# LN on ScalarE, bias loads on another queue, deferred h stores and four late dO products in a transformer block's backward kernel

## The chip, the cores and the metric

The kernel runs on one core of one Trainium2 chip. The metric is the device time of one execution in microseconds, lower is better; it is given as the median of several runs. One further execution is recorded by the hardware profiler, and all profile lines come from it.

## The reference

The kernel computes the forward result and all gradients of a small gated block. With S = 2048 rows, D = 512, 32 heads of 16 and F = 1792, in bfloat16:

```python
xn = layernorm(x)
s = attention(xn; wqkv, wo)                  # 32 heads, full softmax, then @ wo
y = layernorm(xn)
h = gelu(y @ w1 + b1); m = h @ w2 + b2
out = x + s * silu(m)
# outputs: out and the gradients of x, wqkv, wo, w1, b1, w2, b2 for a given grad_out
```

The layer norm is applied twice, so there are two sets of row means and deviations. The gradient that enters the attention is `(grad_out * silu(m)) @ wo.T`; the kernel calls the factor before the product `dso` and the product dO.

## The kernel before

Line numbers are those of the profile. Everything runs in an order that is written out by hand: each engine (and each engine's DMA queue) takes its instructions in program order, and an instruction that has to wait holds up those behind it. There are three phases: `phase_pre` (L38), `attention_core` (L637) and `phase3`. The change touches the first, and the first block of the second. Tensors have 16 row tiles of 128 rows; four tiles make a group.

**QKV stage of `phase_pre`.** SP (SyncE's queue) loads `x_all` in four groups (L74). ACT's queue loads `wqkv` in three parts (L76), w1 (L77), b1 (L78, two-byte elements spread over partitions) and b2 (L79, broadcast to 128 partitions). `stats` takes the moments of a group on DVE (VectorE: L86, L87), the square root on ACT (ScalarE: L89), the reciprocal and -mean/deviation on DVE (L90, L91). `norm` (L96) normalises four tiles on DVE. `ln1(g)` makes `xn` from `x` and transposes it into `xnT`: group 0 through PE (TensorE), the others by a DMA transpose on SP (L111). `ln2(g)` makes `y` from `xn` and a transpose `yT` (L118).

The loop over 16 tiles does, per tile t: three products of `xnT` with `wqkv_sb` (L139), each in one of six PSUM buffers; three casts to SBUF on ACT (L144 to L146) into `NSall` (two buffers of four tiles) and `NQ`; two squares on POOL (GpSimd, L150); then, if t is in `hooks`, one LN step, ln1(2), ln1(3), ln2(0) to ln2(3) after tiles 1, 3, 5, 8, 11, 14; then the reduction of the previous tile's squares on DVE (L125). After every fourth tile SP stores `NSall` and `NQ` to DRAM (`NAT_s`, `NATQq_s`, L157, L158).

**h1.** `h1(sc)` makes the hidden layer for one group: 14 groups of four matmuls (L185), the bias added on DVE into an `h1row` buffer (L188, six buffers), the GELU on ACT into `hgT` (L189), and a store of `h1row` to `H1T_s` on SP (L190). At its end SP stores the whole `hgT`, 1.8 MB, to `HGT_s` (L191). The order is `h1(0)`, load of `w2_sb` (L254), `load_dot(0)` (L178), transposing load of `woT` (L256), `h1(1)`, `load_dot(1)`, `row_bound`, then the sixteen `m_step`s, with `h1(2)` and `h1(3)` after the first and second four.

**`m_step(t)`** has a pipeline of six tiles: transposes of `dso(t-2)` on PE (`dso_tr`, L225) and their copy on ACT (L227), the product with `woT` for tile t-5 (`proj`, L233) and its copy into `ND` on ACT (L235), `gate(t-1)` and `slope_out(t-3)` on DVE and POOL (L206 to L219), and the 14 matmuls of m (L197) for tile t. After tile 15 come the last transposes and `proj(11)` to `proj(15)`.

**Attention.** 16 pairs of heads times four query blocks, 64 blocks, each of 16 steps; the backward half of a block runs during the next block, so the first block has none. A step has scores `s` (L758), `d` (L770), an exponential on ACT (L784), two products on DVE (L802), and the accumulations into `X` (L828, L840, L852); from the second block on also `t` (L744) with its exponential (L792) and `Z` (L924, L936). `eg` buffers rotate by three, each written for four steps and then transposed by a DMA (L813). The pair-0 operands for query tiles 4 to 15 are loaded and transposed during block 0, in steps 1, 3 and 5.

## Time and profile before

| what | us |
|---|---|
| median of four runs | 2346.89 (2340.46 to 2358.44) |
| the profiled execution | 2340.46 |
| its span | 2338.4 |
| PE busy in the span | 2175.6 (93%) |
| ACT busy | 1834.6 (78%) |
| DVE busy | 1805.0 (77%) |
| POOL busy | 1196.5 (51%) |
| attention's first score matmul starts at | 202.72 |

The page divides the span into 40 slices; shares over the whole span are mostly those of the long attention phase. For the first part one has to look at the stretches: a table by stage gives each engine's busy time there, and the clock that the throttle granted to TensorE (1.00 is full speed). A line of the instructions in order of time gives start, duration, engine, source line, operation, output and input; in brackets stand the idle time before it and what ended it. "SPq" and "ACTq" are the DMA issues of these engines, and their time is that of the issue, not of the transfer. PE's busy time is modelled and includes the overlap of neighbouring matmuls.

### The profile page before, as it was taken

To read this page: it belongs to the slowest core of one execution; us is meant where nothing else is said; L and a number is where in the kernel's file an instruction comes from. 1 tells how busy PE (TensorE), PEld (TensorE's weight loads), DVE (VectorE), ACT (ScalarE), POOL (GpSimd) and SP (SyncE) were. 2 spreads that over 40 slices of the span, in tenths; PEclk is the share of its full clock that TensorE was granted. 3 is DMA by queue.
4 is the path that set the end of the run, shared out by engine and by line. 5 is a ranking of instruction groups with operands and counts; after the bars stand their busy time and mean duration, and the time that the engine had idled before them with its cause. 6 is when DMAs were issued, how large, how long until landed. Compare 5 with 4: busy or idle time off the path is not lost.

```text
span 2338.4 us, 47577 instructions
## 1 busy us (share of the span) xinstructions
PE 2175.6 (93%) x18320; PEld 729.8 (31%) x18320; DVE 1805.0 (77%) x3022; ACT 1834.6 (78%) x2131; POOL 1196.5 (51%) x1956
## 2 busy tenths in 40 slices
PE   6799999999999999999999999999999998789997
PEld 2343222222222222222222222222222223234455
DVE  7676698998999899978888998998888994204641
ACT  4555799999999999989999999999998995221231
POOL 4247447566575657465656656474756555200020
PEclk9997699999999999989999999999998999999999
DMA  7867799999999999999999999999999999898556
GB/s 197 246 210 192 179 240 240 236 250 247 230 248 243 242 234 249 245 214 236 245 242 245 248 247 249 245 240 244 243 223 229 239 236 244 213 234 244 163 81 129
DMA packets 1761557, 529.90 MB, mean 227 GB/s; under 512 B 1682337, under 2 KB 1746994, under 8 KB 1761330
## 3 DMA queue, kind: packets, MB, share of 16 engines
q1 hardware_dynamic: 1715858, 467.59, 98.2%
q10 hardware_dynamic: 33152, 31.87, 4.9%
q0 software_dynamic: 12320, 27.41, 4.0%
q8 instruction: 143, 2.34, 0.4%
q14 instruction: 84, 0.69, 0.1%
HBM read 47.98 MB, written 58.33 MB: 45 GB/s over the span
## 4 chain that ended last, share of the span: by engine, by line
PE 51%; ACT 23%; DMA 10%; POOL 6%; DVE 4%; issue 4%; ACTq 1%; SPq 0%; POOLq 0%; DVEq 0%
ACT e L792 11%; ACT eg L784 10%; PE d L770 9%; PE s L758 8%; PE X L828 8%; DMA tg<-eg 5%; PE X L840 4%; PE Z L936 3%; PE X L852 2%; PE ps_dhg L551 2%; PE ps_h L185 2%; PE ps_dy L566 2%; DMA hgc<-HGT_s 1%; PE ps_dw L625 1%; PE ps_m L197 1%
## 5 line engine op out<-in xcount | busy, mean ns | idle before, releaser
L802 DVE TENSOR_TENSOR eg<-d,eg 128x512 bf16<-128x512 f32 x2048 | 1349.5, 688 | 186.0 <-PE d L770 69.8
L784 ACT ACTIVATE eg<-s 128x1024 bf16<-128x1024 f32 x1024 | 1041.3, 1034 | 72.3 <-PE d L770 54.6
L770 PE MATMUL d<-QDT,KVT 32*128 32x512 bf16 x2048 | 807.6, 394 | 0.7 <-DVE eg L802 0.6
L792 ACT ACTIVATE e<-t 128x1024 bf16<-128x1024 f32 x640 | 662.9, 1036 | 44.0 <-PE t L744 41.7
L758 PE MATMUL s<-QDT,KVT 32*128 32x512 bf16 x2048 | 409.6, 395 | 42.2 <-ACT eg L784 39.5
L840 PE MATMUL X<-eg,NAT 128*32 128x512 bf16 x2048 | 414.9, 402 | 0.0
L828 PE MATMUL X<-eg,Lc 128*32 128x512 bf16 x2048 | 414.8, 402 | 0.0
L852 PE MATMUL X<-eg,NAT 128*17 128x512 bf16 x2048 | 407.9, 395 | 0.0
L770 PEld LDWEIGHTS <-KVT 32*128 32x128 bf16 x2048 | 186.0, 91 | 347.2 <-issue 347.2
L924 PE MATMUL Z<-e,W 128*32 128x512 bf16 x1280 | 256.5, 396 | 20.7 <-POOL W L891 19.4
L744 PE MATMUL t<-KVT,QDT 32*128 32x512 bf16 x1280 | 254.5, 391 | 3.1 <-ACT eg L784 2.7
L758 PEld LDWEIGHTS <-KVT 32*128 32x128 bf16 x2048 | 116.8, 91 | 296.2 <-issue 294.4
L936 PE MATMUL Z<-tg,W 128*32 128x512 bf16 x2048 | 207.6, 390 | 0.0
L885 POOL TENSOR_TENSOR W<-NATQd,rL 128x128 bf16<-128x128 bf16 x64 | 25.9, 405 | 350.4 <-DVE rL L869 350.4
L828 PEld LDWEIGHTS <-Lc 128*32 128x32 bf16 x2048 | 98.8, 93 | 285.5 <-issue 285.5
L691 POOL TENSOR_TENSOR bg_v<-bg_t 128x512 f32<-128x512 f32 x56 | 58.0, 1036 | 193.6 <-ACT bg_t L706 193.2
L924 PE MATMUL Z<-tg,W 128*32 128x512 bf16 x768 | 154.5, 399 | 0.0
L840 PEld LDWEIGHTS <-NAT 128*32 128x32 bf16 x2048 | 99.1, 94 | 168.0 <-issue 168.0
L342 POOL TENSOR_TENSOR dx<-lnb_prod,lnb_dy 128x512 bf16<-128x512 f32 x16 | 20.9, 1312 | 233.0 <-DVE lnb_prod L341 233.0
L950 DVE TENSOR_TENSOR acc<-Z,acc 128x512 f32<-128x512 f32 x192 | 130.7, 681 | 10.5 <-PE Z L936 10.5
L924 PEld LDWEIGHTS <-W 128*32 128x32 bf16 x2048 | 108.9, 93 | 47.4 <-POOL W L891 23.7
L852 PEld LDWEIGHTS <-NAT 128*17 128x17 bf16 x2048 | 92.9, 88 | 60.3 <-issue 60.3
(164 smaller groups left out, 2749.4 us busy)
## 6 DMA issues: line engine op xcount, KB each, us to landing
H1T_s<-h1row SPq DMA_DIRECT2D x56, 128.0 KB, 1.8
HGT_s<-hgT SPq DMA_DIRECT2D x4, 1792.0 KB, 7.9
bg_x<-H1T_s POOLq DMA_DIRECT2D x56, 128.0 KB, 5.4
GP_s<-bg_m POOLq DMA_DIRECT2D x56, 128.0 KB, 5.5
gp<-GP_s ACTq DMA_DIRECT2D x8, 896.0 KB, 7.1
DH1T_s<-dh1T SPq DMA_DIRECT2D x4, 1792.0 KB, 9.6
NAT_s<-NSall SPq DMA_DIRECT2D x4, 1056.0 KB, 6.5
NAT<-NAT_s POOLq DMA_DIRECT2D x16, 264.0 KB, 5.9
```

The costliest lines, as they stand in the source:

```text
L744: nc.tensor.matmul(t[:, hj, :], lhsT=op["QDT"][r:r + 32, q0:q0 + 128], rhs=op["KVT"][r:r + 32, kc * 512:(kc + 1) * 512], start=True, stop= ...
L758: nc.tensor.matmul(s[:, hj, :], lhsT=op["KVT"][r:r + 32, kb * 128:(kb + 1) * 128], rhs=op["QDT"][r:r + 32, qc * 512:(qc + 1) * 512], start ...
L770: nc.tensor.matmul(d[:], lhsT=op["KVT"][r:r + 32, kb * 128:(kb + 1) * 128], rhs=op["QDT"][r:r + 32, qc * 512:(qc + 1) * 512], start=True, ...
L784: nc.scalar.activation(out=cur["eg"][1][:, :, kb % 4, :, :].rearrange("k b h q -> k h b q"), in_=st_s.pop(g)[:].rearrange("k h (b q) -> k ...
L792: nc.scalar.activation(out=e[:], in_=st_t.pop(g)[:], func=ACT.Exp)
L802: nc.vector.tensor_tensor(out=gts[:, kb % 4, hj, :].rearrange("k (b q) -> k b q", b=4), in0=ds[hj][:].rearrange("k (b q) -> k b q", b=4), ...
L828: nc.tensor.matmul(X[64 + 32 * hj:96 + 32 * hj, :], lhsT=Lc[:], rhs=et[:, :, kb % 4, hj, :], start=(kb == 0), stop=False, skip_group_check ...
L840: nc.tensor.matmul(X[32 * hj:32 * hj + 32, :], lhsT=NATt[:, kb, hj, 1:33], rhs=et[:, :, kb % 4, hj, :], start=(kb == 0), stop=(kb == 15), ...
L852: nc.tensor.matmul(X[64 + 32 * hj:64 + 32 * hj + 17, :], lhsT=NATt[:, kb, hj, 0:17], rhs=gts[:, kb % 4, hj, :], start=False, stop=(kb == 1 ...
L924: nc.tensor.matmul(Z[32 * hj:32 * hj + 32, :], lhsT=blk[j]["W1"][:, qb, hj, :], rhs=ev[:, hj], start=(i == 0), stop=False, tile_position=( ...
L936: nc.tensor.matmul(Z[c:c + 32, :], lhsT=blk[j]["W2"][:, qb, hj, :], rhs=gv[:, :, hj, qb, :], start=(i == 1), stop=(i >= 2), tile_position= ...
L950: nc.vector.tensor_tensor(out=av, in0=Z[:], in1=av, op=ALU.add)
```

## The change

- `norm_act` normalises on ACT, as `x * rstd + nmr` with both taken per row. It serves all groups of `ln2`, and groups 1 to 3 of `ln1`; group 0 stays on DVE. `ln2` works in place in `xn`, whose buffers go from four to three. The hooks are ln1(2), ln2(0), ln1(3), ln2(1), ln2(2), ln2(3) after tiles 1, 3, 5, 8, 11, 14.
- The loads of b1 and b2 leave ACT's queue. With the loads of `w2_sb` and `woT` they're put on SP after tile 5 of the QKV loop.
- The store of `hgT` becomes `store_h`, called after the next `h1` for groups 0 to 2, and before the last `gate` for group 3. `h1row` has eight buffers; the squares' buffers go from four to three.
- The three 16 KB `eg` buffers of the attention are made before `phase_pre`, each with a name of its own. `phase_pre` uses them first: `x_all`, then `hgT` of groups 0 and 2, in the first; `hgT` of groups 1 and 3 in the second; `w1_sb`, then `late_sb`, in the third. `late_sb` holds a second transposed copy of `wo` (loaded on SP after `h1(3)`), the `ND` buffer and transposes for tiles 12 to 15, and `dso(15)`. `NSall` moves to the pool of the QKV stage.
- `proj(12)` to `proj(15)` and `dso_tr(15)` become a generator `rest` that the attention loop calls in its first steps; they use the PSUM buffer of `Z`. The loads of the pair-0 operands in block 0 move from steps 1, 3, 5 to 7, 9, 11.

```diff
+LATE = 12
...
+        eg_as = lambda i, shape, name: k.egp.tile(shape, bf16, name=name, tag=f"eg{i}")
-        x_all = hp.tile([128, NT, D], bf16, name="x_all", tag="hA")
-        NSall = hp.tile([128, 2, NPAIR, 4, 2, NATW], bf16, name="NSall", tag="hB")
-        w1_sb = hp.tile([128, IC, F], bf16, name="w1_sb")
+        x_all = eg_as(0, [128, NT, D], "x_all")
+        w1_sb = eg_as(2, [128, IC, F], "w1_sb")
...
-            nc.scalar.dma_start(out=b1_bf[:], in_=B_b1.rearrange("(c p) -> p c", p=128))
-            nc.scalar.dma_start(out=b2_bf[:], in_=B_b2.rearrange("(o d) -> o d", o=1).to_broadcast([128, D]))
...
+            def norm_act(dst, src, g, rstd_all, nmr_all):
+                for i in range(4):
+                    t = 4 * g + i
+                    nc.scalar.activation(out=dst[:, i, :], in_=src[:, i, :], func=ACT.Identity, bias=nmr_all[:, t:t + 1], scale=rstd_all[:, t:t + 1])
...
-                xn[g] = p0.tile([128, 4, D], bf16, name="xn", bufs=4)
-                norm(nc.vector, xn[g], src, mv, rs)
+                xn[g] = p0.tile([128, 4, D], bf16, name="xn", bufs=3)
                 if g == 0:
+                    norm(xn[g], src, mv, rs)
...
                 else:
+                    norm_act(xn[g], src, g, k.rstd1, k.nmr1)
...
-                y[g] = p0.tile([128, 4, D], bf16, name="y", bufs=2)
-                norm(nc.vector, y[g], xn[g], mv, rs)
+                norm_act(xn[g], xn[g], g, k.rstd2, k.nmr2)
...
-                    sq = wk0.tile([128, H, DH], f32, name="sq", bufs=4)
+                    sq = wk0.tile([128, H, DH], f32, name="sq", bufs=3)
...
+                if t in hooks:
+                    hooks[t]()
+                if t == 5:
+                    nc.sync.dma_start(out=b1_bf[:], in_=B_b1.rearrange("(c p) -> p c", p=128))
+                    nc.sync.dma_start(out=b2_bf[:], in_=B_b2.rearrange("(o d) -> o d", o=1).to_broadcast([128, D]))
+                    nc.sync.dma_start(out=w2_sb[:], in_=B_w2.rearrange("(c p) d -> p c d", p=128))
+                    nc.sync.dma_start_transpose(out=woT[:], in_=A_wo)
...
-                    h1row = hp.tile([128, 512], bf16, name="h1row", bufs=6)
+                    h1row = hp.tile([128, 512], bf16, name="h1row", bufs=8)
...
+            def store_h(sc):
                 nc.sync.dma_start(out=k.HGT_s[:, sc * 512:(sc + 1) * 512].rearrange("(c p) s -> p c s", p=128), in_=hgs[sc][:])
...
             h1(0)
-            nc.sync.dma_start(out=w2_sb[:], in_=B_w2.rearrange("(c p) d -> p c d", p=128))
             load_dot(0)
-            nc.sync.dma_start_transpose(out=woT[:], in_=A_wo)
             h1(1)
             load_dot(1)
+            store_h(0)
             row_bound()
...
                 if sc + 2 < 4:
                     h1(sc + 2)
+                    store_h(sc + 1)
+                if sc == 1:
+                    late_sb = eg_as(2, [128, 16, IC, 128], "late_sb")
+                    nc.sync.dma_start_transpose(out=late_sb[:, 0:4].rearrange("p b m q -> p b (m q)"), in_=A_wo)
+            store_h(3)
...
-            for t in range(NT - 5, NT - 2):
+            for t in range(NT - 5, LATE):
                 proj(t)
-            dso_tr(NT - 1)
-            proj(NT - 2)
-            proj(NT - 1)
+
+            def rest(psum):
+                proj(LATE, psum([128, 512], f32))
+                yield
+                dso_tr(NT - 1, psum([128, IC, 128], bf16))
+                yield
+                for t in range(LATE + 1, NT):
+                    proj(t, psum([128, 512], f32))
+                    yield
+            return rest
...
-    late += [(1, lambda: ops0["load_d"](4, NT)), (3, lambda: ops0["cq"](4, NT)), (5, lambda: ops0["tq"](4, NT))]
+    late += [(7, lambda: ops0["load_d"](4, NT)), (9, lambda: ops0["cq"](4, NT)), (11, lambda: ops0["tq"](4, NT))]
+    rest = rest_of_pre(lambda shape, dt: ps_z.tile(shape, dt, name="Z0", tag="z"))
     emit_s(0)
     emit_exp_a(0)
...
+        if g < 7:
+            next(rest, None)
```

## The prediction

> **What bounds the kernel now.** I read four views in this order: the table by stage, the instructions in order of time over the first 112 us, the chain of work that ended last around 200 us, and the instructions of single tiles for durations. The profiled execution took 2340.46 us around a span of 2338.4 us; the median of the four runs is 2346.89 us, 6.4 us above it. All sums below are differences against the profiled execution and are then taken off the median.
>
> The first stretches are, in order: query/key/value (QKV) and LN, the two first `h1`, the sixteen `m_step`, attention block 0, block 1, block 2. Columns: PE, weight loads, DVE, ACT, POOL busy us with counts, then granted clock, DMA share, GB/s.
>
> ```profile
> 17.50:77.70 60.20, 50.59 (x233) 23.11 (x234) 56.29 (x141) 30.33 (x62) 32.33 (x32) 1.00 0.68 156
> 77.70:108.70 31.00, 22.13 (x89) 9.29 (x89) 16.98 (x25) 15.54 (x25) 0.45 (x1) 0.84 0.93 281
> 108.70:198.00 89.30, 87.90 (x450) 40.86 (x449) 67.18 (x94) 49.13 (x81) 52.22 (x54) 1.00 0.67 212
> 198.00:240.00 42.00, 39.02 (x192) 8.07 (x189) 25.01 (x38) 25.39 (x31) 20.07 (x26) 0.61 0.85 193
> 240.00:279.70 39.70, 39.70 (x248) 8.15 (x249) 24.80 (x38) 27.67 (x30) 13.98 (x25) 0.51 0.75 173
> 279.70:306.00 26.30, 25.79 (x253) 7.71 (x254) 24.06 (x39) 25.48 (x29) 13.46 (x25) 1.00 1.06 212
> ```
>
> QKV is bound by DVE (56.29 of 60.20). The `h1` stretch is bound by nothing that computes: PE works 22 of 31 us. The `m_step` stretch is bound by PE. Blocks 0 and 1 run at about half clock with PE full; block 1 takes 39.7 us where block 2 takes 26.3.
>
> ```profile
> 6.56 9.39 ACTq L79 DMA_DIRECT2D b_bf<-in_B_b_dram  x1
> 8.77 0.18 DVE L87 BATCH_NORM_AGGREGATE ln_mv<-ln_st 128x2 f32<-128x6 f32 x1
> 15.98 1.28 ACT L89 ACT_TABLE_LOAD   x1 [15.98 <-issue]
> 20.51 1.91 PE L139 MATMUL pk<-wqkv_sb,xnT 128*128 128x512 bf16 x4
> ...
> 90.27 4.71 SPq L178 DMA_DIRECT2D dot<-in_grad_out_dram  x1
> 95.03 7.07 SPq L256 DMA_TRANSPOSE woT<-in_A_wo_dram  x1
> 104.80 5.36 DVE L188 TENSOR_SCALAR h1row<-ps_h,b1c 128x512 bf16<-128x512 f32 x8 [12.39 <-DMA H1T_s<-h1row]
> 105.60 3.22 PE L185 MATMUL ps_h<-yT,w_sb 128*128 128x512 bf16 x8 [8.87 <-DVE h1row L188]
> ```
>
> Two stalls stand out. ACT issues the b2 load until 15.95, while its statistics were ready at 8.95. And SP is held by the dot and `woT` issues from 90.3 to 102.1, the `H1T_s` stores queue behind them, six `h1row` buffers run out, and PE stands for 8.87 us; its next eight matmuls take 0.40 us each instead of 0.216.
>
> **The change, part by part.**
>
> **Bias loads off ACT.** The Sqrt waits only for the statistics: end 9.4 instead of 17.58. The steps from there to the first QKV matmul take 20.51 - 17.58 = 2.9, so it starts at 12.3: 8.2 us earlier. Its inputs are there: the three `wqkv_sb` loads land within 5.4 to 8.0 us of issues that end at 2.4.
>
> **LN normalised on ACT.** Seven of eight groups leave DVE: 7 x 1.38 = 9.7 us. The nearest ACT row is the same form:
>
> ```profile
> L515 ACT ACTIVATE y_all<-xn_all,nmr,rstd x16: 797/799/814, 2070.1 to 2114.7; 128x512 bf16<-128x512 bf16 x16
> 2070.08 2.22 ACT L515 ACTIVATE y_all<-xn_all,nmr,rstd 128x512 bf16<-128x512 bf16 x3 [0.45 <-ACT dw_out L511]
> ```
>
> Three take 2.22, so 0.71 apart and 2.93 for four. The Trainium skill (ScalarE: Activation LUTs, Rules for kernel authors) says to keep multiply and add on VectorE, which is up to three times as fast; here 2.93 against 1.38, a factor of 2.1. By the rule the edit loses 7 x 1.55 = 10.9 us if ACT sets the pace; by DVE's busy row it gains 9.7. Neither is right alone, because ACT runs in order: the eviction casts of the next tile stand behind the four norms, and the norms behind the statistics. So I laid the stage out by hand, with these durations: QKV group on PE 0.863 (2.59 a tile), casts 0.485 apart (1.5 a tile), squares on POOL 1.04 each, reductions 0.59 each, statistics 3.17 a group, Sqrt 0.3, reciprocal and product 0.5.
> - Hooks at tiles 1, 3, 5 (two tiles apart): ACT needs 6 casts 3.0 + 0.8 + 2.93 = 6.7 us per hook, so it sets the pace. The norm groups start at 22.0, 28.7 and 35.6 (before: 29.1, 36.7, 44.3): 7 to 9 us ahead. The third waits for `yT(0)` to leave `xn`'s reused buffer; it lands at 31.6 + 0.3 + 3.7 (issue to landing of these transposes) = 35.6, just in time.
> - Hooks at 8, 11, 14 (three apart): a loop closes. Casts 1.5, squares and reduction behind them 1.9, statistics 3.2, Sqrt to product 1.0, norms 2.93, with small steps 10.5 us. Before, the norms lay on DVE, ACT went on at once, and the period was DVE's 8.8. The norms start at 46.1, 56.4, 66.8 (before 53.1, 61.9, 70.7): the lead falls from 8.7 to 3.9.
> - End: norms until 69.7, casts of tile 15 until 71.2, +1.9 reduction, +1.6 for biases and maximum: first `h1row` at 74.7 instead of 76.9. **The gain that remains is 2.2 us.** Bounds: +11 where the casts slip past the waits (PE then sets 12.3 + 41.5 plus some 10), -4 where each loop is 2 us longer. I take 2.2. Fewer `sq` buffers (3 for 4) cost nothing in this layout, since the reduction that frees them comes before the next square.
>
> **SP's burst at tile 5.** It puts b1, b2, `w2_sb`, `woT` on SP after `xnT(3)`, at about 40.3. Before, the issues took 0.37, 9.39, 1.74 and 7.07, each behind full traffic; DMA moved 74 GB/s at 30 to 40 us and 281 at 40 to 50. I take half for the two long ones, 9 to 10 us in all. Then the `NAT_s` store of tiles 4 to 7 goes at 50 and lands 6.5 to 9 later, 57 to 59; the cast of tile 12, which reuses that buffer, is due at 59.3. Cost 0, up to 12 if all four take their old issue times (18.6) and the stores behind theirs.
>
> **`h1` without the SP stall.** `w2_sb` and `woT` are gone from this place and the 1.8 MB store of h(0) comes after h1(1). The stores alone took 10.02 us for 14, inside PE's 12.1. So 8.87 + 1.6 (eight matmuls at 0.40 for 0.216) = 10.5 us go. Eight `h1row` buffers only add cover. About 0.8 more, half of the like cold start at 77.7, since PE's wait there splits into two of about 2.5 us. The deferred stores go where others went; only h(3)'s comes new to the end, beside attention's start, and must land before step 4 writes that buffer (7.9 us after its issue, about 10 are there): 0.
>
> **The second `woT` transpose** goes behind h(2)'s store, in the PE-bound stretch. Behind it on SP: `NATQd_s`, `DSO_s` and `GB_s` stores; three `dso` and four `gB` buffers give some 8 us. In the profile SP already stood 4.7 there. 0 to 5; I take 1.
>
> **Four products inside block 0.** At the seam:
>
> ```profile
> 197.77 1.28 ACT L267
> 199.27 0.47 ACT dsoT L227
> 199.74 1.46 ACT ND L235 x3
> 201.20 0.50 ACT dsoT L227
> 201.75 1.05 PE pd L233 x4
> 203.30 1.04 ACT eg L784
> ```
>
> The first exponential no longer waits for the last products: table until 199.05, a copy to 199.8, one `ND` copy to 200.3, so 2.9 us earlier. But four copies of 0.6, one of 0.57, 16 matmuls and 4 transposes come back between steps 0 and 4. At full clock, step 5's exponential starts at 208.2 instead of 211.0: -2.8. At half clock each of those steps costs PE 4 x 0.427 = 1.7 more, and step 5 starts about 5 later. With no row to decide, I take 0 between them. The moved pair-0 loads (steps 1, 3, 5 to 7, 9, 11) still precede block 1 by several steps: 0.
>
> The clock itself is the large unknown. The Trainium skill (TensorE: Matmul & The Clock Gate, Part 1) says that about 3.4 us of sustained activity bring back the full clock. The `h1` start agrees (half clock from 77.7 to 80.7). Block 0 does not: PE was busy all the time from 207 to 279 and stayed at 0.50. By the rule blocks 0 and 1 would lose 2 us to it, and there would be nothing to win; by the row they lose some 24 (13.4 in block 1, 16 steps at about 2.2 us for DVE's 1.4 in block 0). Dense products could wake it. I take 0.
>
> **Sum:** 2.2 + 10.5 + 0.8 - 1 + 0 = 12.5, rounded to 13: 2346.9 - 13 = 2334 us (the profiled execution's 2340 would be 2327).
>
> **The rivals.**
> - *ACT does not hold QKV up:* PE and DVE take the 8.2 us through and DVE's 9.7 count; another 11: 2323. For: ACT was busy only 30 of 60 us. Against: the loop above.
> - *The clock comes back in block 0:* dense full-array products at half clock wake it, as the dense `h1` products did within some 3 us at 77.7 and 105.6; 8 us in block 0 and 12 in block 1: 2314. For: 1.7 us of dense work per step. Against: block 0's transposes at 240.0 did not wake it, and from step 5 on the mix is what let it fall.
> - *SP's burst takes its old issue times:* `NAT_s` lands at 71 for 59, all of QKV's end shifts by 12: 2346, no change. For: the 9.39 of b2 directly behind b1's two-byte elements. Against: less traffic.
> - *Slower:* the half clock lasts longer. PE stands from 198.8 to 202.0 behind ACT's copies, the clock falls some 5 us before the products (+5), and it stays down through blocks 2 and 3 as well: each costs 39.7 - 26.3 = 13.4. 12.5 - 5 - 26.8 = -19: 2366. It decides from about 37 us more of half clock on (12.5 over the 34% it costs). For: it lasted 71 us before. Against: later falls lasted 3 to 14 us.
>
> **How the numbers follow.** Chances: forecast 0.48 (own range 2326 to 2343), ACT no bound 0.10, clock back 0.19, burst 0.13, longer half clock 0.10. 0.5% is 11.7 us, about what a measurement of this kernel can tell from no change (its four runs spread over 0.8%), so the bound is 2335.2 and the forecast lies next to it. Faster: 0.26 of the forecast's 0.48, and the first two rivals, 0.55. Slower than 2358.6 by that bound: most of the last rival, and what it has with the burst, 0.09. The rest, 0.36, is the same. The range runs from 2310 (under the clock rival) to 2350 (over the burst) and leaves out the last rival and the clock rival's far end.
>
> **What would show it.** In the profile after: first QKV matmul at about 12; ACT, not DVE, before the waits of QKV, with norm groups 6.7 and then 10.5 apart; first `h1row` near 75; no PE gap of 8 us in `h1`, the first `ps_m` near 95; attention's first exponential near 187; granted clock 0.5 in most of blocks 0 and 1. It is wrong if `h1row` starts under 68 or over 80, if SP's burst holds the cast of tile 12, or if the half clock's length differs by more than 20 us from 71.

## The result and the profile after

The changed kernel takes 2357.65 us (median of 43 runs, 2326.56 to 2394.0), the kernel before 2372.31 us (median of 68 runs, 2338.55 to 2425.12). The ratios given here compare only those runs of each kernel that lie within 1.5% of its fastest (24 of the 43 and 39 of the 68, medians 2348.21 and 2360.24 us): 0.9949, with a 95% interval of 0.9926 to 0.9971, or about 12 us less (7 to 18). The medians of all runs are 14.7 us apart. So the forecast difference of 13 us came out, and the forecast time of 2334 us did not: it stood on a median of 2346.89 us from four runs, and the kernel before takes 25 us more than that in the middle of 68. The measured time lies above the range's upper end of 2350.

The time goes with the clock granted to TensorE, which differs from one execution to the next. Over the 208 runs of all kernels below for which the clock is known (one at 2910.37 us and a clock of 0.556 left out), a run's time falls by 1614 us per unit of mean clock within one kernel (16.1 us for 0.01), and what is left scatters by 2.4 to 4.2 us. So two comparisons are given below: the measured ratio, and the *difference at equal clock*, for which each run is first moved to a mean clock of 0.95 with that slope (in brackets, two standard errors). For the change it is -7.8 us (1.5). The rest of its 12 to 15 us goes with a mean clock of 0.9505 for 0.9467 (72 runs of the kernel before beside the experiments), worth 0.0038 x 1614 = 6.1 us, with a standard error of 2.7.

The profiled execution of the changed kernel took 2365.2 us (span 2363.0, clock 0.944). The table by stage, with the stages that answer to those of before (QKV, h1, `m_step`, blocks 0, 1, 2); columns as before:

```profile
9.30:74.10 64.80, 51.65 (x233) 23.32 (x234) 48.08 (x113) 49.40 (x90) 32.50 (x32) 1.00 0.91 227
74.10:94.80 20.70, 20.70 (x89) 9.07 (x89) 18.66 (x26) 16.34 (x26) 0.45 (x1) 0.92 0.76 231
94.80:186.30 91.50, 88.56 (x445) 40.80 (x444) 66.58 (x92) 47.65 (x78) 51.85 (x53) 0.98 0.65 209
186.30:232.00 45.70, 38.62 (x195) 8.82 (x195) 24.72 (x38) 25.95 (x32) 20.30 (x26) 0.66 0.91 220
232.00:264.90 32.90, 32.40 (x242) 7.90 (x242) 23.98 (x38) 26.09 (x29) 13.98 (x25) 0.70 0.90 187
264.90:291.10 26.20, 25.63 (x249) 7.67 (x249) 23.87 (x39) 25.57 (x29) 13.48 (x25) 1.00 1.16 237
```

QKV now has no full engine (DVE 48 and ACT 49 of 65 us). In h1, PE has no idle time left once it has restarted at 74.1. The stretch of block 0 has become longer, 45.7 us for 42.0, with 7 us in which PE does nothing. The instructions in order of time, up to attention:

```profile
9.09 0.30 ACT L89 ACTIVATE rstd<-ln_mv,eps_t 128x4 f32<-128x4 f32 x1 [4.51 <-DVE ln_mv L87]
12.33 1.91 PE L144 MATMUL pk<-wqkv_sb,xnT 128*128 128x512 bf16 x4
40.95 0.89 SPq L161 DMA_DIRECT2D b_bf<-in_B_b_dram  x1
42.36 8.84 SPq L163 DMA_TRANSPOSE woT<-in_A_wo_dram  x1
73.30 6.94 DVE L198 TENSOR_SCALAR h1row<-ps_h,b1c 128x512 bf16<-128x512 f32 x10
94.77 5.56 PE L209 MATMUL ps_m<-w_sb,hgT 128*128 128x512 bf16 x25
149.88 6.99 SPq L288 DMA_TRANSPOSE late_sb<-in_A_wo_dram  x1
161.64 0.68 DVE L218 TENSOR_TENSOR gB<-m_bf,sg 128x512 bf16<-128x512 bf16 x1 [3.57 <-DMA GB_s<-gB]
189.19 1.02 ACT L812 ACTIVATE eg<-s 128x1024 bf16<-128x1024 f32 x1
```

The first QKV matmul, the first `h1row` and the first `ps_m` stand within 1.4 us of where they were forecast (12.3, 74.7, 95). The lead over before is 3.6, then 13.9, then 14.1 us at the first exponential (12.0 in the second pair of profiles, below). The second load of `wo` holds SP for 7 us, and DVE waits 3.57 us for a `GB_s` store behind it. Then, in block 0:

```profile
201.68 4.91 SPq L841 DMA_TRANSPOSE tg<-eg  x1
206.69 0.53 SPq L255 DMA_DIRECT2D NATQd_s<-late_sb  x1
211.40 2.85 ACT L812 ACTIVATE eg<-s 128x1024 bf16<-128x1024 f32 x3 [5.29 <-DMA NATQd_s<-late_sb]
212.47 0.61 PE L786 MATMUL s<-QDT,KVT 32*128 32x512 bf16 x2 [3.89 <-ACT eg L812]
```

Step 8 writes its exponentials into the third `eg` buffer, which is `late_sb`. The late `ND` in it is still being stored, since the store stood on SP behind the first transpose of `eg` (201.68 to 206.59). The same wait stands in e2 (6.32 us) and e8 (5.67), which keep `ND` there. The same stretch by windows of 2 us (busy times of PE, weight loads, DVE, ACT, POOL, then granted clock):

```profile
206.00:208.00 2.00, 2.00 (x20) 0.60 (x16) 1.76 (x3) 0.10 (x1) 0.00 (x0) 1.00 1.02 232
208.00:210.00 2.00, 0.58 (x5) 0.19 (x5) 0.00 (x0) 0.00 (x0) 0.00 (x0) 1.00 1.09 244
210.00:212.00 2.00, 0.00 (x0) 0.00 (x0) 0.00 (x0) 0.60 (x1) 0.28 (x1) 0.73 1.28 212
212.00:214.00 2.00, 1.41 (x5) 0.21 (x4) 1.40 (x3) 2.00 (x3) 1.97 (x3) 0.50 1.28 290
```

While PE waits the clock falls to half, and it stays there until 252. Before that, it had fallen at the seam, where `phase_pre` ends and attention begins (190.4), and come back at 200.7, amid the late products. The transposes that end block 0 (`XT`) come at 232.03, so that of the 14.1 us 8.0 are left.

The markers of all kernels (us; one profile each, so that the clock in blocks 0 and 1 is that of one execution), and the times; "first exp." is attention's first exponential:

| kernel | first h1row | first ps_m | first exp. | XT of block 0 | of block 1 | ratio to before | at equal clock |
|---|---|---|---|---|---|---|---|
| before | 76.88 | 108.66 | 203.30 | 240.00 | 279.13 | 1 | 0 |
| the same, second profile (e12) | 77.04 | 109.23 | 204.48 | 241.91 | 271.67 | | |
| changed | 73.30 | 94.77 | 189.19 | 232.03 | 264.91 | 0.9949 (0.9926 to 0.9971) | -7.8 (1.5) |
| the same, second profile (e13) | 73.16 | 94.63 | 192.44 | 232.27 | 259.32 | | |
| e1 ND in tg | 73.38 | 94.84 | 192.27 | 236.83 | 275.99 | 1.0003 (0.9955 to 1.0051) | -2.1 (2.1) |
| e2 norms on DVE | 72.75 | 94.23 | 191.27 | 231.32 | 264.19 | 0.9994 (0.9945 to 1.0043) | -8.0 (1.7) |
| e3 no late products | 73.31 | 93.09 | 187.00 | 221.38 | 255.20 | 0.9942 (0.9905 to 0.9978) | -14.7 (1.9) |
| e5 bias loads alone | 69.01 | 101.36 | 196.93 | 234.07 | 261.33 | 0.9993 (0.9942 to 1.0044) | -7.3 (1.8) |
| e6 ND in Oall | 73.33 | 93.12 | 190.46 | 225.92 | 257.25 | 0.9905 (0.9848 to 0.9961) | -9.1 (1.8) |
| e7 no late products, norms on DVE | 71.12 | 90.91 | 184.77 | 221.84 | 249.16 | 0.9867 (0.9827 to 0.9908) | -15.9 (2.0) |
| e8 wo copied on the chip | 73.17 | 92.95 | 185.14 | 226.85 | 256.65 | 0.9937 (0.9896 to 0.9978) | -12.5 (2.1) |
| e9 whole change, mended | 72.01 | 91.79 | 183.97 | 221.01 | 260.21 | 0.9929 (0.9884 to 0.9974) | -13.4 (2.5) |
| e10 as e7, wo at tile 12 | 68.72 | 92.36 | 186.94 | 218.06 | 249.40 | 0.9896 (0.9842 to 0.9950) | -16.6 (3.1) |
| e11 as e9, loads split | 68.72 | 90.19 | 184.39 | 217.85 | 251.19 | 0.9847 (0.9799 to 0.9896) | -18.0 (2.1) |

The code up to the first `ps_m` is the same in the changed kernel, e1, e3, e6 and e8. Their first `h1row` agrees within 0.2 us, but the first `ps_m` stands at 92.95 to 94.84, as the half clock of some 3.4 us in h1 begins at 74 or 75 us in some (changed, e13, e1) and at 69 or 70 in the others. So 2 us between single profiles say nothing there.

### The profile page after: what moved, and what is told of

Its sections match the earlier page's. It is cut to its first block, busy times and chain, and to the rows that moved or that the text cites. A ratio compares the mean times of both kernels' runs of the same rounds, so it can differ in the third digit from the quotient of the medians.

```text
span 2363.0 us, 47583 instructions
## 1 busy us (share of the span) xinstructions
PE 2209.2 (93%) x18320; PEld 733.2 (31%) x18320; DVE 1799.8 (76%) x2994; ACT 1856.3 (79%) x2159; POOL 1196.4 (51%) x1956
## 4 chain that ended last, share of the span: by engine, by line
PE 53%; ACT 22%; DMA 8%; POOL 6%; issue 4%; DVE 3%; ACTq 0%; POOLq 0%; SPq 0%; DVEq 0%
ACT e L820 10%; PE d L798 10%; ACT eg L812 9%; PE s L786 9%; PE X L856 9%; PE X L868 5%; PE Z L964 3%; PE X L880 3%; DMA tg<-eg 3%; PE ps_dy L596 2%; PE ps_dhg L581 2%; PE ps_m L209 2%; DMA hgc<-HGT_s 1%; PE ps_dw L539 1%; PE ps_dw L655 1%
## 5 line engine op out<-in xcount | busy, mean ns | idle before, releaser
L798 PE MATMUL d<-QDT,KVT 32*128 32x512 bf16 x2048 | 819.6, 401 | 0.1
L786 PE MATMUL s<-QDT,KVT 32*128 32x512 bf16 x2048 | 416.1, 401 | 45.0 <-ACT eg L812 39.8
L868 PE MATMUL X<-eg,NAT 128*32 128x512 bf16 x2048 | 420.9, 408 | 0.0
L856 PE MATMUL X<-eg,Lc 128*32 128x512 bf16 x2048 | 420.7, 408 | 0.0
L880 PE MATMUL X<-eg,NAT 128*17 128x512 bf16 x2048 | 413.7, 401 | 0.0
L952 PE MATMUL Z<-e,W 128*32 128x512 bf16 x1280 | 261.4, 404 | 20.8 <-POOL W L919 19.4
L964 PE MATMUL Z<-tg,W 128*32 128x512 bf16 x2048 | 211.4, 397 | 0.0
L952 PE MATMUL Z<-tg,W 128*32 128x512 bf16 x768 | 156.8, 405 | 0.0
L978 DVE TENSOR_TENSOR acc<-Z,acc 128x512 f32<-128x512 f32 x192 | 130.7, 681 | 10.5 <-PE Z L964 10.5
L952 PEld LDWEIGHTS <-W 128*32 128x32 bf16 x2048 | 109.1, 93 | 47.9 <-POOL W L919 23.7
```

The source lines that it names most:

```text
L786: nc.tensor.matmul(s[:, hj, :], lhsT=op["KVT"][r:r + 32, kb * 128:(kb + 1) * 128], rhs=op["QDT"][r:r + 32, qc * 512:(qc + 1) * 512], start ...
L798: nc.tensor.matmul(d[:], lhsT=op["KVT"][r:r + 32, kb * 128:(kb + 1) * 128], rhs=op["QDT"][r:r + 32, qc * 512:(qc + 1) * 512], start=True, ...
L856: nc.tensor.matmul(X[64 + 32 * hj:96 + 32 * hj, :], lhsT=Lc[:], rhs=et[:, :, kb % 4, hj, :], start=(kb == 0), stop=False, skip_group_check ...
L868: nc.tensor.matmul(X[32 * hj:32 * hj + 32, :], lhsT=NATt[:, kb, hj, 1:33], rhs=et[:, :, kb % 4, hj, :], start=(kb == 0), stop=(kb == 15), ...
L880: nc.tensor.matmul(X[64 + 32 * hj:64 + 32 * hj + 17, :], lhsT=NATt[:, kb, hj, 0:17], rhs=gts[:, kb % 4, hj, :], start=False, stop=(kb == 1 ...
L952: nc.tensor.matmul(Z[32 * hj:32 * hj + 32, :], lhsT=blk[j]["W1"][:, qb, hj, :], rhs=ev[:, hj], start=(i == 0), stop=False, tile_position=( ...
```

## The experiments

**The front: what did ACT's norms cost?** The theory was that moving the norms to ACT gave back most of the 8 us of the early start. First the bias loads alone, put into the kernel before:

```diff
-            nc.scalar.dma_start(out=b1_bf[:], in_=B_b1.rearrange("(c p) -> p c", p=128))
-            nc.scalar.dma_start(out=b2_bf[:], in_=B_b2.rearrange("(o d) -> o d", o=1).to_broadcast([128, D]))
...
+                if t == 5:
+                    nc.sync.dma_start(out=b1_bf[:], in_=B_b1.rearrange("(c p) -> p c", p=128))
+                    nc.sync.dma_start(out=b2_bf[:], in_=B_b2.rearrange("(o d) -> o d", o=1).to_broadcast([128, D]))
```

> The kernel before with one edit of the change alone: the loads of b1 and b2 leave ScalarE's queue and go on SyncE's behind the LN of tile 5. Theory (ACT held by the issue of b2 until 16 us was all that delayed the start, and DVE sets the pace from there): first QKV matmul at 12.3 us, DVE full until the first h1row at 68.7 us, the stall of the h1 stage stays at 8 to 10 us, the first ps_m at about 100.5 us for 108.7; 6 to 8 us shorter than the kernel before. Rival (the issue of b2 costs on SyncE what it cost on ScalarE): SP stands 9 us behind b2 at 40 us, a NAT_s store comes late, the casts of tile 8 or 12 wait for it, and the first h1row is at 75 us or later.

In order of time, with the h1 stage that this kernel still has unchanged:

```profile
69.01 4.04 DVE L189 TENSOR_SCALAR h1row<-ps_h,b1c 128x512 bf16<-128x512 f32 x6
97.23 5.36 DVE L189 TENSOR_SCALAR h1row<-ps_h,b1c 128x512 bf16<-128x512 f32 x8 [12.64 <-DMA H1T_s<-h1row]
98.04 3.49 PE L186 MATMUL ps_h<-yT,w_sb 128*128 128x512 bf16 x8 [9.12 <-DVE h1row L189]
101.36 1.89 PE L198 MATMUL ps_m<-w_sb,hgT 128*128 128x512 bf16 x8
```

The theory's numbers hold to 0.9 us: 12.49 for the first matmul, 69.01, a stall of 9.12, 101.36. So the bias loads alone give 7.9 us at the first `h1row`, where the whole change has 3.6, and -7.3 us (1.8) at equal clock, as much as the whole change. The measured ratio, 0.9993, cannot tell it from 1: its interval is half a percent, or 12 us, to each side. Next, in the changed kernel, the norms back on DVE:

```diff
-                    norm_act(xn[g], src, g, k.rstd1, k.nmr1)
+                    norm(xn[g], src, mv, rs)
...
-                norm_act(xn[g], xn[g], g, k.rstd2, k.nmr2)
+                norm(xn[g], xn[g], mv, rs)
```

> The changed kernel with the seven later LN groups normalised on VectorE as before (LN2 in place in xn), everything else as changed. Theory (ACT's in-order queue, not DVE's busy time, sets the pace of the changed QKV stage, so that moving the norms cost what the early start gained): DVE is full again, the periods fall to the 8.8 us of before, the first h1row starts at 68.7 us (76.9 less the 8.2 us of the earlier start) where the changed kernel has 73.3, and the later stages start 4 to 5 us earlier. Rival (DVE's load was the limit and taking it off helped): the first h1row starts at 76 us or later, and the time rises by 3 us or more.

Neither came. The first `h1row` starts at 72.75, only 0.55 earlier, and there's no difference at equal clock. The first of two other limits shows in the order of time:

```profile
67.76 1.04 POOL L155 TENSOR_TENSOR sq<-NQ 128x512 f32<-128x512 bf16 x1 [3.70 <-DVE kn L130]
72.75 7.81 DVE L198 TENSOR_SCALAR h1row<-ps_h,b1c 128x512 bf16<-128x512 f32 x11
```

POOL waits for one of the three `sq` buffers, which DVE frees late now that it norms between the reductions. The next kernel therefore has four again, with the norms on DVE, all dO products ahead of attention (no `late_sb`, no second load of `wo`), and the late pair-0 loads at steps 1, 3 and 5; of these edits only the buffers and the norms lie ahead of the first `h1row`:

```diff
-                    sq = wk0.tile([128, H, DH], f32, name="sq", bufs=3)
+                    sq = wk0.tile([128, H, DH], f32, name="sq", bufs=4)
...
-            for t in range(NT - 5, LATE):
+            for t in range(NT - 5, NT - 2):
                 proj(t)
+            dso_tr(NT - 1)
+            proj(NT - 2)
+            proj(NT - 1)
...
-    late += [(7, lambda: ops0["load_d"](4, NT)), (9, lambda: ops0["cq"](4, NT)), (11, lambda: ops0["tq"](4, NT))]
+    late += [(1, lambda: ops0["load_d"](4, NT)), (3, lambda: ops0["cq"](4, NT)), (5, lambda: ops0["tq"](4, NT))]
```

> The changed kernel without its last part (all dO products ahead of attention, no second wo load, late loads of pair 0 back at steps 1, 3 and 5), with the later LN groups normalised on VectorE in place, and four sq buffers again. What stays of the change: bias loads off ScalarE's queue, w2 and wo loaded at tile 5, deferred h stores, xn in place. Theory (the gain of the change is the 8 us of the bias loads and the 10 us of the h1 stall; ACT's norms and the seam gave it back): first h1row at 69.0 us, first ps_m at 90 us, first exponential at 184 us, no wait for QDT at block 1; at the same mean clock 18 to 22 us shorter than before, 11 to 14 shorter than the changed kernel. Rival (the front's time is hidden behind what follows, so that an earlier start of attention only meets its loads): first exponential as above, but a wait for KVT, QDT or a tg in block 0 or 1 takes 5 us or more back; 12 to 15 us shorter than before.

The first `h1row` is at 71.12 now, 1.6 better and still 2.1 behind e5, though POOL still waits with four buffers (the last time 2.71 us, at 67.06). In order of time:

```profile
42.18 8.54 SPq L163 DMA_TRANSPOSE woT<-in_A_wo_dram  x1
50.82 0.53 SPq L167 DMA_DIRECT2D NAT_s<-NSall  x1
57.51 0.60 ACT L149 CAST NSall<-pk 128x512 bf16<-128x512 f32 x1 [3.29 <-DMA NAT_s<-NSall]
```

This is the second limit: the burst on SP, for which no cast waits in the changed kernel's profile, makes the cast of tile 12 wait 3.29 us once the norms no longer hold it up. At equal clock the kernel is 15.9 us (2.0) faster than before and 8 faster than the changed one, between the theory's 18 to 22 and the rival's 12 to 15; the rival's wait of 5 us in blocks 0 and 1 did not come. Moving the `woT` load from tile 5 to tile 12 takes most of this limit away (the wait for `NAT_s` is 1.31 us):

> The version with all products ahead of attention and the norms on VectorE once more, with one difference: the transposing load of wo goes on SyncE's queue at tile 12 instead of tile 5. Theory (at tile 5 it kept the NAT_s store of tiles 4 to 7 back until 50.8 us, so that the cast of tile 12 waited 3.3 us): no cast waits for a store, no PE gap of 3.6 us at 58 us, first h1row at 69.0 us for 71.1, first exponential at 182.7 us for 184.8; 2 us shorter at the same mean clock, 17 to 19 shorter than before. Rival (the load at tile 12 keeps yT of the last group back and h1 meets it, or its store burst): first h1row at 69 but a stall in h1, first ps_m at 91 us as it was, no gain.

The first `h1row` starts at 68.72, as forecast. But the rival's stall in h1 came:

```profile
61.21 6.14 SPq L164 DMA_TRANSPOSE woT<-in_A_wo_dram  x1
72.29 9.89 SPq L201 DMA_DIRECT2D H1T_s<-h1row  x14
77.79 4.70 DVE L199 TENSOR_SCALAR h1row<-ps_h,b1c 128x512 bf16<-128x512 f32 x7 [3.72 <-DMA H1T_s<-h1row]
214.32 1.94 ACT L804 ACTIVATE eg<-s 128x1024 bf16<-128x1024 f32 x2 [6.32 <-DMA tg<-eg]
```

The load pushes `yT` and the last `NAT_s` stores back, the first `H1T_s` store goes 3.6 us after its row, and h1 stalls on its buffers: the first `ps_m` is at 92.36, later than e7's 90.91. So the three limits of QKV (ACT's norms, three `sq` buffers, SP's burst) stood behind each other. Taking them away one after the other moved the first `h1row` by 0.55, 1.6 and 2.4 us. In e10 the last 2.4 were lost again in h1; e11, with the same front, has the stall too (3.21 us) but its `ps_m` at 90.19, so part of the loss is the clock's. The last line is a new wait, in block 0: its clock stayed full from the seam to 212 us, and ACT came to a buffer whose transpose had not ended. At equal clock e10 and e7 cannot be told apart.

**The late products.** The kernel as changed, but with all products ahead of attention, and without `late_sb` and the second load of `wo`. It differs from e7 in ACT's norms, three `sq` buffers and the late loads at 7, 9, 11; the edit is the middle part of e7's.

> The changed kernel with the last four dO products and the last transpose of dso back ahead of attention, without late_sb and without the second transposing load of wo; the late loads of pair 0 stay at steps 7, 9, 11. Theory (the second wo load costs about 4 us ahead of attention, the seam gains about 3, and the dense products bring the clock back in block 0 at 200 us): no DVE wait of 3.6 us and no PE gap near 162 us; first exponential near 189 us (4 earlier for the load, 3 to 5 later for the products, which stand before it again); block 0 falls to half clock within 8 us of its start and stays there for 40 us or more, so that its transposes come 33 to 40 us after the first exponential. Rival (the products inside block 0 cost more than they give): the first exponential as above, no half clock longer than in the changed kernel, and a time 3 to 8 us shorter than the changed kernel's.

At equal clock it is 14.7 us (1.9) faster than before, so the late products and what belongs to them cost the changed kernel 6.9 us (about 2.3). No gap stands near 162 us, and the first exponential is at 187.00, 2.2 us earlier than with the products moved. But 1.7 of these are there at the first `ps_m` already; from there it takes 93.9 us, where the changed kernel takes 94.4 and 97.8 (e13). So the second load of `wo` took back at least what the move gained. Half clock came at 206, not within 8 us of the start, and lasted 37.5 us where the changed kernel's two falls make 51.2: it's the rival that holds. And a wait that nobody had on the list stands at block 1's first scores, for the operand that the loads moved to steps 7, 9 and 11 bring:

```profile
215.47 0.61 PE L777 MATMUL s<-QDT,KVT 32*128 32x512 bf16 x2 [4.20 <-DMA QDT<-Pad]
```

Then each part alone. The `ND` outside of `late_sb`, in a tile of attention's `tg` rotation:

```diff
-                nd = ND[(t // 4) % 2] if t < LATE else late_sb[:, 4:8].rearrange("p b m q -> p (b m q)").rearrange("p (a b c) -> p a b c", a=NPAIR, b=4)
+                nd = ND[(t // 4) % 2] if t < LATE else nd_late
...
+    nd_late = tgp.tile([128, 48, 128], bf16, name="tg")[:, 0:16, :].rearrange("p m q -> p (m q)").rearrange("p (a b c) -> p a b c", a=16, b=4)
```

> The changed kernel with one difference: the last four dO products write their natural copy ND into a tile of attention's tg rotation instead of into late_sb, so that step 8's eg buffer has no store to wait for. Theory (late_sb's store makes step 8 wait, and the gap lets the clock fall a second time): the exponential of step 8 no longer waits 5.3 us for the NATQd_s store, steps 4 to 11 run in about 1.3 us each, the transposes of block 0 move from 232.0 to at most 226.5 us, and if the clock then stays up to 220 us at least, block 1's move from 263 to under 252 us; the time falls by 5 to 15 us against the changed kernel. Rival (the thin matmul mix of block 0 lets the clock fall whether or not there is a gap): the wait goes, but half clock begins within 5 us of 210 us and lasts some 40 us all the same; the time falls by 0 to 5 us.

The edit made a wait of its own:

```profile
201.81 0.58 ACT L253 CAST tg<-Z 128x512 bf16<-128x512 f32 x1 [8.53 <-DMA NATQd_s<-ND]
230.91 0.61 PE L786 MATMUL s<-QDT,KVT 32*128 32x512 bf16 x2 [5.43 <-DMA QDT<-Pad]
```

That `tg` lies on memory that the store of the previous `ND` still reads, and ACT stands 8.53 us with the exponentials behind it. The time is 5.7 us worse than the changed kernel's and says nothing on the theory. The clock does: step 8 no longer waits, and the full clock, back at 207, holds past 210 until 228, where PE stands 5.43 us for `QDT`. Once more with `ND` in the part of `Oall` that block 3 is the first to write:

```diff
+    nd_late = Oall[:, 12:16, :].rearrange("p t d -> p (t d)").rearrange("p (a b c) -> p a b c", a=16, b=4)
```

> The changed kernel with the late ND copy in the part of Oall that is first written at block 3, instead of in late_sb (and instead of in tg, whose memory the store of the ND before it still reads). Theory A (the store in eg2 is what costs block 0): no exponential of block 0 waits for a store, steps 4 to 11 run at 1.3 us each, block 0 takes 5 us or more less than the 42.8 us of the changed kernel, and the whole is 4 us or more shorter at the same mean clock. Theory B (the late loads are the next in the row): step 8 does not wait, but the NATQd store still stands behind the first tg transpose on SP until about 207 us, the query operand QDT for block 1 comes some 7 us behind its issue after the second tg, and the first s of block 1 waits 3 to 6 us for QDT<-Pad, the clock falls in that gap; the gain is 0 to 4 us at the same mean clock.

```profile
205.12 0.53 SPq L255 DMA_DIRECT2D NATQd_s<-Oall  x1
216.58 1.39 SPq L345 DMA_TRANSPOSE QDT<-Pad  x1
220.01 0.61 PE L786 MATMUL s<-QDT,KVT 32*128 32x512 bf16 x2 [6.25 <-DMA QDT<-Pad]
```

```profile
212.00:214.00 2.00, 1.77 (x15) 1.00 1.44 189
214.00:216.00 2.00, 0.00 (x0) 1.00 1.03 276
216.00:218.00 2.00, 0.00 (x0) 0.67 0.11 26
218.00:220.00 2.00, 0.00 (x0) 0.50 1.13 256
```

The first fence is in order of time, the second shows windows with PE's busy time and the clock. Both theories are right in part. The wait at step 8 is gone and block 0 takes 35.5 us for 42.8. But the next wait is there at once: the store of `ND` goes at 205.12, the operand built from it is issued at 216.58, and block 1's first scores wait 6.25 us; PE is idle, and the clock falls in that gap. At equal clock the gain on the changed kernel is 1.3 us (about 2): theory B's.

The second load of `wo` replaced by a copy on the chip:

```diff
-                    nc.sync.dma_start_transpose(out=late_sb[:, 0:4].rearrange("p b m q -> p b (m q)"), in_=A_wo)
+                    nc.sync.dma_start(out=late_sb[:, 0:4].rearrange("p b m q -> p b (m q)"), in_=woT[:])
```

> The changed kernel with one difference: late_sb gets wo's transpose by a plain copy from woT on the chip instead of a second transposing load from HBM. Theory (the transposing issue holds SP's queue some 7 us, GB_s and DSO_s stores stand behind it, DVE and PE wait): no DVE wait of 3 us or more near 161 us, no PE gap and no half clock near 162 us, first exponential at 185 us for 189.2, 3 to 5 us shorter at the same mean clock. Rival (the gain is taken back at the seam): first exponential at 185 us, but block 0 longer by the same amount.

```profile
148.05 2.79 SPq L288 DMA_DIRECT2D late_sb<-woT  x1
159.29 0.69 DVE L218 TENSOR_TENSOR gB<-m_bf,sg 128x512 bf16<-128x512 bf16 x1 [3.05 <-DMA GB_s<-gB]
160.49 0.40 PE L238 MATMUL tp_ps<-ident_bf,dso 128*128 128x128 bf16 x4 [1.81 <-DVE dso L220]
```

DVE's wait is not gone (3.05 us), but PE's gap is down from 2.32 to 1.81 and there's no half clock beside it. The first exponential is at 185.14, and 4.7 us (about 2.4) are won on the changed kernel at equal clock. From the first `ps_m` to the first exponential it takes 92.2 us. With the transposing load that stretch took 94.4 in the changed kernel and 97.8, 97.4, 97.0 and 97.3 in e13, e1, e2 and e6: the load costs 2.2 us in one profile and 4.8 to 5.6 in four. Without late products it takes 93.9 in e3 and e7, so the move itself gains 1.7 us ahead of attention (e9 also has 92.2; but e11 for e10 only 94.2 for 94.6).

**All of it mended.** `ND` in `Oall`, `wo` copied, norms on DVE with four `sq` buffers, and the late store on GpSimd's queue:

```diff
-                    nc.sync.dma_start(out=k.NATQd_s[:, :, t - 3:t + 1, :].rearrange("a p t c -> p a t c"), in_=nd[:] if t < LATE else nd)
+                    (nc.sync if t < LATE else nc.gpsimd).dma_start(out=k.NATQd_s[:, :, t - 3:t + 1, :].rearrange("a p t c -> p a t c"), in_=nd[:] if t < LATE else nd)
```

> The changed kernel with all its parts, each mended where it cost: ND in Oall as in the other run, its late store issued from GpSimd's queue so that it doesn't stand behind the tg transposes, wo's transpose copied on the chip, norms on VectorE with four sq buffers. Theory A (dense products inside block 0 keep the clock up once nothing makes PE wait): first exponential at 181 us, block 0 under 30 us, block 1 at 27 us, 25 us or more shorter than before at the same mean clock, and shorter than the version without the late products. Theory B (the late products bring nothing even then): first exponential at 181 us, but QDT comes late for block 1 as the store of NATQd comes only after step 5, the clock falls in that gap; no shorter, or up to 5 us longer, than the version with all products ahead of attention.

Theory B: `QDT` still comes late (4.89 us, at 215.10), the clock falls in that gap for 51.2 us, and at equal clock the kernel is 2.5 us behind e7, too little to tell. The first exponential was 3 us later than forecast, as SP's burst holds QKV up here too. Last, the same with the loads split, so that block 1's operands don't depend on the late products, and with the `woT` load at tile 12:

```diff
-    late += [(7, lambda: ops0["load_d"](4, NT)), (9, lambda: ops0["cq"](4, NT)), (11, lambda: ops0["tq"](4, NT))]
+    late += [(1, lambda: ops0["load_d"](4, 12)), (3, lambda: ops0["cq"](4, 12)), (5, lambda: ops0["tq"](4, 12)),
+             (7, lambda: ops0["load_d"](12, NT)), (9, lambda: ops0["cq"](12, NT)), (11, lambda: ops0["tq"](12, NT))]
```

> The mended version of the whole change, with the wo load at tile 12 and the late loads of pair 0 split: tiles 4 to 11 of dO, which don't depend on the late products, go at steps 1, 3, 5 as before, and only tiles 12 to 15 at 7, 9, 11, which block 3 is the first to need. Theory A (what lets the clock fall in blocks 0 and 1 is a PE gap of 4 us and more, and the dense products bring it back from the one at the seam): no wait for QDT at block 1, half clock for at most 10 us at the seam and none after it in blocks 0 and 1, block 0 (first exponential to its transposes) 32 us or less, block 1 at 27 us; 20 to 25 us shorter than before at the same mean clock, 5 or more shorter than the version with the products ahead. Theory B (the late products cost in block 0 what they save ahead of it): first exponential 2 us earlier than the version with the products ahead, block 0 longer than that by 2 us or more at equal share of half clock, and no time gained over it.

No wait for `QDT` is left, and the fall at the seam lasts 10.2 us. But a second one follows at 217, for 20.5 us, after a gap of 1.32 us behind ACT, which had waited 2.40 us for `tg<-eg` (windows with PE's busy time and the clock):

```profile
212.00:214.00 2.00, 2.00 (x16) 1.00 0.92 236
214.00:216.00 2.00, 0.68 (x7) 1.00 0.29 66
216.00:218.00 2.00, 1.79 (x11) 0.69 0.85 195
```

Block 0 takes 33.5 us and block 1 33.3, for the 32 and 27 expected by theory A. Against e10, theory B's numbers hold: the first exponential is 2.6 us earlier and block 0 2.3 us longer, though the clock's falls differ. The wait for `tg` is a further one in the row: e3, e10 and e11, which came through much of block 0 at full clock, have it (2.60, 6.32 and 2.40 us) and lost the clock in that gap or just behind it. In before, e12, e5 and e7, at half clock there, no exponential waits for it. Full clock alone does not decide it, as e9 has only 0.69 us of it and e6 none. At equal clock it's 18.0 us (2.1) faster than before, against 15.9 (2.0) and 16.6 (3.1) for e7 and e10 with the products ahead of attention. So the late products, with their own waits mended, bring at most a few microseconds, and these runs don't tell that from nothing. By the measured ratio this is the fastest version, 0.9847 (0.9799 to 0.9896), with e7 (0.9867) inside its interval. Both beat the kernel before and the changed one.

**What is the kernel's, and what the one execution's?** Both kernels, unchanged, profiled a second time:

> The kernel before, unchanged, profiled a second time, to see what of blocks 0 and 1 belongs to the kernel and what to the one execution. Theory (the clock's falls follow the kernel's own gaps and are the same each time): half clock again from about 206 us for about 72 us, the transposes of blocks 0 and 1 again at 240 and 279 us, within 2 us. Rival (the fall comes at the seam each time, but its length differs by tens of microseconds from one execution to the next): first exponential at 203 us as before, half clock from 206 us, but for another length, as in the run with the bias loads alone (38 us), and block 1 at 27 us for 39.

> The changed kernel, unchanged, profiled a second time. Theory (the stalls are the kernel's): DVE's wait near 161 us and the wait of step 8's exponential again, each within 1.5 us of 3.6 and 5.3; first exponential at 189 us within 1.5. Rival (they are chance meetings of transfers): one of them under 1 us or over 8. For the clock: if its falls follow the gaps, half clock again in the gap before step 8, from about 210 us; its length may differ.

Windows of the kernel before, second profile (PE's busy time and the clock):

```profile
202.00:206.00 4.00, 2.34 (x13) 1.00 0.31 120
206.00:208.00 2.00, 1.49 (x11) 0.85 0.66 186
208.00:212.00 4.00, 4.00 (x22) 0.50 1.18 275
248.00:252.00 4.00, 4.00 (x30) 0.53 0.77 185
252.00:256.00 4.00, 4.00 (x38) 1.00 0.78 179
```

The fall comes at 207 again, but lasts 44.4 us instead of 71.7, so that block 1 takes 29.8 us for 39.1: the rival. The changed kernel, second profile, in order of time:

```profile
150.90 6.43 SPq L288 DMA_TRANSPOSE late_sb<-in_A_wo_dram  x1
164.07 0.43 DVE L218 TENSOR_TENSOR gB<-m_bf,sg 128x512 bf16<-128x512 bf16 x1 [6.13 <-DMA GB_s<-gB]
211.65 2.85 ACT L812 ACTIVATE eg<-s 128x1024 bf16<-128x1024 f32 x3 [6.11 <-DMA NATQd_s<-late_sb]
```

Both stalls are there again, so they're the kernel's, but their size isn't fixed: DVE's wait is 6.13 for 3.57, outside the 1.5 us that the theory allowed, and the first exponential is 3.3 us later for it. The clock falls in the gap again, at 211.6 (210.9 the first time), for 23.9 us instead of 41.0; the fall at the seam is missing this time.

## Why the prediction was right or wrong

- **The base, which made the time wrong.** The step that failed is the last one of the sum, "then taken off the median": the median of the four runs, 2346.89, was taken as the time of the kernel before, and the range held nothing for it. Over 68 runs it's 2372.31. These 25.4 us are more than the whole miss of 23.7 (2357.65 - 2334). For the profiled one of the four the difference goes with the clock: it took 2340.46 us at a mean clock of 0.963, the second profile of the same kernel 2371.84 at 0.944, and 0.019 x 1614 = 31 us is the whole difference. The first had 15 falls of 3.4 to 71.7 us, 174 us in all, the second 18 with 266; had their lengths been taken as chance, the range would have had to reach some 30 us further up. The clock of the other three isn't on record. Nor is it shown why the four go together: only 10 of the other 64 runs are as short as the longest of them, so that four such draws in a row would be a rare chance.
- **Bias loads: right.** Forecast 12.3 us for the first QKV matmul, measured 12.33.
- **Norms on ACT: right in mechanism and nearly in size.** The norm groups were forecast at 22.0, 28.7, 35.6, 46.1, 56.4 and 66.8 us and started at 21.66, 28.27, 35.12, 45.37, 55.59 and 65.81; the first `h1row` gained 3.6 us for the forecast 2.2. The Trainium skill's rule (ScalarE: Activation LUTs, Rules for kernel authors) that multiply and add belong on VectorE spoke against the edit. By e2 alone it makes no difference here (0.55 us at `h1row`); with the other two limits gone, QKV with the norms on DVE ends 4.6 us earlier (68.72 for 73.30). Fewer `sq` buffers and SP's burst were put at 0. For the burst that holds in the changed kernel, where no cast waits for it; the buffers were not tried there alone. With the norms on DVE the two come due, at 1.6 and 2.4 us.
- **h1: right.** Forecast 11.3 us (10.5 + 0.8); the stage went from 31.8 to 21.5 us, and from 32.2 to 21.5 in the second profiles, 10.3 and 10.7. (The stall's part of the sum is 10.4 rather than 10.5: eight matmuls at 0.40 for 0.216 make 1.5.) So the 0.8 for half of the cold start did not show. e5, which has none of the edits in h1, keeps the stall (9.12 us); which of them removes it, the moved loads, the deferred store or the eight buffers, was not tried apart.
- **The second `woT` transpose: undersized.** Taken as 1 of a range of 0 to 5; it measured 2.2 in one profile and 4.8 to 5.6 in four, against the copy on the chip. The "some 8 us" of buffer cover did not reach: behind SP's 7 us of issue stand an `ND` and a `DSO_s` store, and the first `GB_s` store goes at 158.85, 9 us after the load's start.
- **Products inside block 0: the mechanism was incomplete.** "I take 0 between them" failed. Ahead of attention the move gained 1.7 us or less, not 2.9, and block 0, from the first exponential to its transposes, grew from 36.7 and 37.4 to 42.8 and 39.8 us. The price of the reused `eg` buffers was worked out for the second one (h(3)'s store before step 4) and not for the third, where step 8 waits for the store of `late_sb`. The moved pair-0 loads, put at 0 because they "still precede block 1 by several steps", cost 4.2 us in e3 and 6.25 in e6; in the changed kernel step 8's wait hides them.
- **The clock: put at 0, and the rival's mechanism came in part.** Where the clock fell at the seam, it was back after 6.8 to 10.2 us in four profiles with late products in block 0 (changed, e8, e9, e11) and after 13.7 in a fifth (e1, where PE stood idle for 8.9 of them). In the four with the products ahead (before, e12, e5, e7) it came back after 37.6 to 71.7 us. That speaks for dense products that wake it, though other edits differ between the two groups. But in each of the five the next gap put it down again, so that little was won. The prediction's own sign, a length more than 20 us off 71, came: 51.2 us in blocks 0 and 1 of the changed kernel, and 23.9 the second time. Its last rival reads the seam wrong: PE did not stand from 198.8 to 202.0 but worked 2.6 of the 4 us from 198 to 202.
- **The difference: right in part by luck.** At block 0's transposes the two pairs of profiles give 8.0 and 9.6 us, and all runs at equal clock 7.8, where the sum said 12.5: 5 us were lost in the last part of the change. The measured 12 us contain a higher mean clock as well. Whether the change raises it (its falls come elsewhere) or chance does, at 6.1 us with a standard error of 2.7, is open; without it the forecast 13 us would have been missed by 5.

## What to carry to other kernels

When a buffer is lent to an earlier phase, price every reader that can still hold it at the moment of its first new write, and the place on the queue of the store that frees it; once that wait is mended, look at once for the next one behind it. Where several limits stand behind each other, undoing one alone shows almost nothing, so undo them one on top of the other. And where the granted clock varies, compare runs by time and clock together, and don't take the median of a few runs for the kernel's time.

## What the runs showed of the hardware

In blocks 0 and 1 of the 14 profiles, the clock fell to half in every PE gap of more than 3.8 us that began at full clock (nine gaps, 3.88 to 8.92 us). That agrees with the Trainium skill's page (TensorE: Matmul & The Clock Gate, HAM oscillation), which warns of idle gaps of more than about 3.4 us. But so long a gap was not needed. The clock also fell after gaps of 1.70 us (e3) and 1.32 us (e11). At the seam it fell after one of 2.42 us in five profiles (changed, e1, e8, e9, e11) and not in three (e13, e2, e6), and after 8 us with PE at some 67% and no gap over 0.91 us in four (before, e12, e5, e7) and not in two (e3, e10).

Unexpected was how long it stays down with PE modelled as full: 71.7 and 44.4 us for the same kernel at the same place, 41.0 and 23.9 for the other, all near multiples of 3.4 us (21, 13, 12 and 7 of them). The return after some 3.4 us of sustained work, which the page's Part 1 gives, is not what the thin matmuls of block 0 show. One microsecond at half clock costs 0.34 us on average over the kernel: 0.01 of mean clock is 23.5 us of lost clock, or 47 us at half speed, in a run of 2350 us, for 16.1 us of time.

The issue of one and the same load has no fixed price. b2's took 9.39 us right behind other loads on ACT's queue and 0.89 on SP at 41 us; the transposing load of `wo` took 8.84, 8.54, 6.99, 6.43 and 6.14 us in five cases, and held its queue that long each time, while the copy on the chip took 2.79.
